# Conversion, sums and split of the second MLP's weights as one operation in seven pieces; block weights of one part per unit

## The chip, the cores and the metric

One core of one Trainium2 chip runs the whole program. The metric is device time in microseconds (us) of one execution, median of the runs; lower is better.

## What is computed

```python
x = attention(q, k, v, g_norm)            # 4608 tokens x 512
h = np.maximum(x @ w_in, 0)               # 512 x 2048
x = (s * (h * h) + b) @ w_out             # 2048 x 512
h = max(x @ w1, x @ w2, x @ w3)           # each 512 x 768
out = h @ w_out2                          # 768 x 512
```

All weights are given in 64-bit floats, everything else in 32 bits. Tokens are worked in tiles of 512 (DM and TW in the code).

## The kernel before

**Arithmetic.** A product of 32-bit numbers is made of three TensorE products of parts: each factor is split into `hi` (ACT, a copy that rounds, L179) and `lo` (DVE, factor minus hi, L180), and hi*hi, hi*lo, lo*hi are summed in PSUM. Most of the large products use Strassen's seven products in place of eight. For these the weights are combined beforehand: of four blocks `raw` come four sums `com`, and the seven blocks are split and kept as one tile of 1792 KB (`wc`).

**Weights.** A weight arrives as `raw`, 512 KB of 64-bit words for 128x512 numbers. `w_float` (L183) makes a 32-bit number of it in six instructions: ACT L187 (absolute value of the high word), DVE L188 (clamp), L189 (shift), L190 (sign), L194 (low word), L196 (sum). `plain_op` (L569) is load, these six, and a store of 256 KB to the array `wf_dr` in DRAM. `combine` (L597) with `maker` (L610) loads two such arrays back into `F`, makes the sums into `G` (L616, four instructions of 128x256), splits the seven blocks, and stores them to `wc_dr`, or keeps them. So a combined weight of the second MLP (MLP2) goes through DRAM twice. There are 24 conversions, nine combined weights `com` 0 to 8 of w1, w2, w3 and three `out` 0 to 2 of w_out2.

**Stages**, in us of the profiled execution. The opening, to about 275: attention and the first MLP (MLP1) of the first tiles by plain products, while MLP1's weights come in. To 331: a rim tile. Then three pairs of tiles (`PAIRS`): each has eight units of an H phase (`h_steps`, which makes h and squares it) and then the second product: pair 0 331 to 471 and 471 to 515 (`Second.run`), pair 1 515 to 671 and to 707, pair 2 707 to 826 and to 889. In pair 2 the second product is Strassen's as well (`Blocks.run`), with weights that `block_op` (L1528 on) makes beforehand in the H phase: F is hi plus lo of two stored chunks `wo` (L1534), G four sums (L1537), four splits, and stores to `ws_dr`; five blocks of 256 KB for each of eight q. From 889: MLP2 in units `v1` (nine for each of the token groups SUPERS) and `Output`.

**Order.** The program is written out as a sequence; a counter `clock` is moved on by `tick` as TensorE work is emitted, and `beside_of(fns, a, b)` spreads the functions fns evenly over ticks a to b from now. A store goes out a number of ticks after its data (`store(dst, src, n)`). Within `in_order` instructions keep the written order on each engine; otherwise a scheduler sets it. `U` is the length of a second product, `V` of an H phase in ticks, `ONE` that of one chunk. Loads and stores are all issued by SP, in order, and SP stands at a load whose buffer is not free.

**Preparation** is one list, `prep.todo`, worked off by `prep.step`, each step one whole operation, the load of the next one ahead of it: four steps in the rim tile, six in pair 0's H phase (MLP1's own combined weights, `pair_op`), five in pair 0's Second, 17 over pair 1, and the last four (com 0 to 2, out 2) in pair 2. `inside.step` makes com 3 to 8, out 0 and out 1, one in each unit of MLP2's first group. `block_op` runs as a whole at ticks 37 to 47 of a unit, twice in unit 0. All of these take their buffers F, G, raw and tab from one pool of three (`w2p["p"]`); `w2p["f"]`, with eleven, holds smaller tiles.

**Engines in a unit.** PE's banks are copied by ACT (`a`, `p`, `u`, `b`, all L714), which also squares in part (L460, L463) and makes gh (L483); DVE makes r (L468), the operands ops of Blocks (L1615) and gl (L484). The loads `gb` (squares from `g_dr`) feed gh in `Second.run`.

Of the kernel before, what the change touches and what calls it, by code (L numbers as in the profile page):

```python
# [22 lines left out]
P = 128  # L23
# [48 lines left out]
def fused_kernel(ctx, tc, qt, kv, kvr, g_norm, w_in, w_out, s, b, w1, w2, w3, w_out2, out):  # L72
# [110 lines left out]
    def w_float(raw, ta, tb, by_act=False, to=None):  # L183
# [3 lines left out]
        nc.scalar.activation(out=af, in_=high.bitcast(F32), func=ACTF.Abs)  # L187
# [3 lines left out]
        if by_act:  # L191
            nc.scalar.activation(out=ta, in_=low, func=ACTF.Copy, scale=2.0 ** -29)
        else:
            nc.vector.tensor_scalar(out=ta, in0=low, scalar1=2.0 ** -29, scalar2=None, op0=ALU.mult)  # L194
        to = tb if to is None else to
        nc.vector.tensor_tensor(out=to, in0=tb, in1=ta, op=ALU.add)  # L196
# [372 lines left out]
    def plain_op(src, dst, turned=False):  # L569
        got = {}  # L570

        def load():
            got["raw"] = four("raw")
            if turned:
                n = DM // Q // (P // Q)
                cut = "p (g i a) -> p g i a", "p (i g a) -> p g i a"
                to, come = (x.rearrange(c, g=n, i=P // Q) for x, c in zip((got["raw"], src), cut))
                for g in range(n):
                    dma(out=to[:, g], in_=come[:, g])
            else:  # L580
                dma(out=got["raw"], in_=src)

        def make():
            t = work("tab")
            store(dst, w_float(got["raw"], t[:, :DM], t[:, DM:], to=got["raw"][:, :DM]), 18)

        return load, make
# [22 lines left out]
    def maker(got, tile_of, dst):  # L610

        def make():
            raw, com, (tgt, whole) = got["raw"], blocks(work("G")), tile_of()

            def tt(o, x, y, op):
                nc.vector.tensor_tensor(out=com[:, o], in0=x, in1=y, op=op)  # L616

            tt(0, raw[:, 0], raw[:, 1], ALU.add)
            tt(1, com[:, 0], raw[:, 2], ALU.subtract)
            tt(2, raw[:, 3], com[:, 1], ALU.subtract)  # L620
            tt(3, raw[:, 2], raw[:, 0], ALU.subtract)
            cut = ((0, 3, raw[:, 1:4]), (3, 6, com[:, 0:3]), (6, 7, com[:, 3:4])) if whole is None else ((0, 3, raw[:, 1:4]), (3, 7, com))
            for i, (t, (a, e, src)) in enumerate(zip(tgt, cut)):
                t = t()
                hilo(t[:, 0], t[:, 1], src)
                if whole is None:
                    store(dst[:, :, a:e], t.bitcast(F32), 12 + 3 * i)
            if dst is not None and whole is not None:
                store(dst, whole.bitcast(F32), 18)

        return make
# [129 lines left out]
    big = {}  # L761
    wq = {}

    def v1(si, q, w):
# [42 lines left out]

        x = bank("x")
# [4 lines left out]
        p7 = copy(fpool("p7")[:, :n], d)  # L813
        prod(w, T, x, S2, "t2", False, False, end)
        u2 = copy(fpool("u2")[:, :n], x)
        prod(w, T, d, A22, "t4", False, False, end)
        c21 = sum_of(d, u2, "c21")
        prod(w, T, x, S1, "t1", False, False, end)
        b = copy(bank("b"), x)
        c22 = sum_of(x, p7, "c22")  # L820
        prod(w, T, a, A12, "b21", False, False, end)
        pair(keys[0], a, keys[2], c21)
        some()

# [674 lines left out]
    def com_op(i):  # L1499
        def tile_of():  # L1500
            if i < 3:
                return com_tile()
            wm[i] = t = wc_tile("wb" if i % 3 == 2 else "wa")
            return (lambda: t[:, :, 0:3], lambda: t[:, :, 3:7]), t

        (ja, ma), (jb, mb) = sides_of(i)
        return combine([wf_dr[jb][mb], wf_dr[ja][ma]], tile_of, wc_dr[i])

    def com_tile():
        return [com_part, com_part, lambda: w2p["f"].tile([P, 2, 1, HW], F32R, tag="f", name="hl")], None  # L1510

    def com_part():
        return w2p["cp"].tile([P, 2, 3, HW], F32R, tag="hl", name="hl")

    def out_op(c):
        srcs = [wf_dr[3][2 * c + k][:, o:o + HW] for o in (HW, 0) for k in range(2)]
        def tile_of():
            if c == KC - 1:
                return com_tile()
            wq[c] = t = wqp.tile([P, 2, 7, HW], F32R, tag="wq", name="wq")  # L1520
            return (lambda: t[:, :, 0:3], lambda: t[:, :, 3:7]), t

        return combine(srcs, tile_of, wo_dr.get(c))

    def block_op(q):
        with in_order():
            block_make(q)

    def block_make(q):
        raw, com = blocks(four("F")), blocks(work("G"))  # L1530
        fa, fb = wo[2 * q], wo[2 * q + 1]
        for i, w in enumerate((fa, fb)):
            hi, lo = (w[:, z].bitcast(F32).rearrange("p (n c) -> p n c", c=HW) for z in range(2))
            nc.vector.tensor_tensor(out=raw[:, 2 * i:2 * i + 2], in0=hi, in1=lo, op=ALU.add)  # L1534

        def tt(o, x, y, op):
            nc.vector.tensor_tensor(out=com[:, o], in0=x, in1=y, op=op)  # L1537

        tt(0, raw[:, 1], raw[:, 3], ALU.add)
        tt(1, com[:, 0], raw[:, 0], ALU.subtract)  # L1540
        tt(2, raw[:, 2], com[:, 1], ALU.subtract)
        tt(3, raw[:, 0], raw[:, 1], ALU.subtract)
        own = raw.bitcast(F32R)
        for k, to in enumerate((2, 0, 4, 1)):
            t = w2p["f"].tile([P, 2, HW], F32R, tag="f", name="ws") if k < 2 else own[:, 2 * k - 4:2 * k - 2]
            hilo(t[:, 0], t[:, 1], com[:, k])
# [4 lines left out]
    def wq_ops(ms):  # L1551
        return [plain_op(chunk((w1, w2, w3, w_out2)[j], m), wf_dr[j][m], j == 3) for m in ms for j in range(4)]

    conv = wq_ops(range(KM))
    prep.todo += [pair_op(0), conv[0], pair_op(1), conv[1]]
    prep.todo += [pair_op(i) for i in range(2, QF)] + conv[2:]
    com, outs = [com_op(i) for i in range(NQ)], [out_op(c) for c in range(KM // 2)]
    prep.todo += [*com[:3], outs[2]]
    inside = Ahead()
# [342 lines left out]
```

## Time and profile before

| | us |
|---|---|
| median of 3 runs | 1416.7 (1412.68 to 1416.85) |
| the profiled execution | 1415.81, span 1414.0 |
| PE, PEld busy | 1371.1, 1125.0 |
| DVE, ACT, POOL busy | 1000.4, 775.1, 10.7 |
| DMA | 310.63 MB, 63.5% of 16 engines |
| mean granted clock of PE | 0.992 |

PE is TensorE's matmuls, PEld its weight loads, which lie beside them. DVE, ACT, POOL are VectorE, ScalarE and GpSimd. The span goes from the first to the last instruction. Counts (x38) are of instructions that start in a stretch.

### The profile page before, as it was taken

To read this page: it belongs to the slowest core of one execution; us is meant where nothing else is said; L and a number is where in the kernel's file an instruction comes from. 1 tells how busy PE (TensorE), PEld (TensorE's weight loads), DVE (VectorE), ACT (ScalarE), POOL (GpSimd) and SP (SyncE) were. 2 spreads that over 40 slices of the span, in tenths; PEclk is the share of its full clock that TensorE was granted. 3 is DMA by queue.
4 is the path that set the end of the run, shared out by engine and by line. 5 is a ranking of instruction groups with operands and counts; after the bars stand their busy time and mean duration, and the time that the engine had idled before them with its cause. 6 is when DMAs were issued, how large, how long until landed. Compare 5 with 4: busy or idle time off the path is not lost.

```text
span 1414.0 us, 19588 instructions
## 1 busy us (share of the span) xinstructions
PE 1371.1 (97%) x6822; PEld 1125.0 (80%) x6822; DVE 1000.4 (71%) x1863; ACT 775.1 (55%) x1503; POOL 10.7 (1%) x40
## 2 busy tenths in 40 slices
PE   8999999999999999998988989999999999999998
PEld 6878788877888888776866767888998888888886
DVE  7998866679675776666767779598674575567555
ACT  7975554667776556664456666455453443334332
POOL 1000000000000000000000000000000000000000
PEclk9999999999999999999999999999999999999999
DMA  8486544486767857778458888558684563563542
GB/s 299 149 256 202 192 125 159 159 296 238 254 242 258 280 164 258 254 239 305 156 201 321 285 294 304 225 212 301 235 302 133 202 228 113 195 245 110 184 154 60
DMA packets 153241, 310.63 MB, mean 220 GB/s; under 512 B 62646, under 2 KB 85686, under 8 KB 144182
## 3 DMA queue, kind: packets, MB, share of 16 engines
q1 hardware_dynamic: 153136, 309.38, 63.5%
q8 instruction: 54, 0.88, 0.3%
q14 instruction: 45, 0.37, 0.1%
q10 hardware_dynamic: 6, 0.00, 0.0%
HBM read 213.91 MB, written 95.42 MB: 219 GB/s over the span
## 4 chain that ended last, share of the span: by engine, by line
PE 71%; DVE 11%; DMA 10%; ACT 4%; issue 3%; SPq 1%; DVEq 0%; POOL 0%; ACTq 0%; POOLq 0%
PE x L498 17%; PE d L498 12%; PE y L498 11%; PE o L498 9%; PE b L498 6%; PE a L498 5%; PE h L427 5%; DMA wf_dr<-raw 2%; DMA gb<-g_dr 2%; PE h L155 2%; DVE tb L155 2%; PE y L155 1%; DMA raw<-in_w_out 1%; DMA ws_dr<-F 1%; PE ops L347 1%
## 5 line engine op out<-in xcount | busy, mean ns | idle before, releaser
L498 PE MATMUL y<-gh,w 128*128 128x512 f32 x720 | 238.5, 394 | 5.6 <-ACT gh L483 4.0
L498 PE MATMUL x<-t,wc 128*128 128x512 f32 (+1 forms) x828 | 202.4, 379 | 6.6 <-ACT u L714 5.5
L498 PE MATMUL d<-t,wc 128*128 128x512 f32 (+1 forms) x828 | 201.7, 379 | 7.0 <-ACT p L714 6.3
L498 PEld LDWEIGHTS d<-t,wc 128*128 128x128 f32 x828 | 148.9, 189 | 37.8 <-ACT p L714 8.0
L498 PEld LDWEIGHTS x<-t,wc 128*128 128x128 f32 x828 | 148.6, 189 | 37.2 <-ACT u L714 6.3
L498 PEld LDWEIGHTS y<-gh,w 128*128 128x128 f32 x720 | 136.0, 190 | 35.0 <-ACT gh L483 5.5
L498 PE MATMUL y<-gl,w 128*128 128x512 f32 x360 | 142.0, 394 | 0.7 <-DVE gl L484 0.7
L498 PE MATMUL b<-b,wc 128*128 128x512 f32 (+1 forms) x414 | 101.8, 381 | 3.5 <-ACT b L714 3.3
L779 DVE TENSOR_TENSOR c<-d,u 128x512 f32<-128x512 f32 (+1 forms) x45 | 28.7, 637 | 106.2 <-PE d L498 106.2
L498 PE MATMUL a<-b,wc 128*128 128x512 f32 (+1 forms) x414 | 101.0, 376 | 0.0
L498 PE MATMUL x<-b,wc 128*128 128x512 f32 (+1 forms) x414 | 100.1, 376 | 0.0
L498 PEld LDWEIGHTS b<-b,wc 128*128 128x128 f32 x414 | 74.7, 190 | 20.4 <-ACT b L714 6.5
L498 PEld LDWEIGHTS x<-b,wc 128*128 128x128 f32 x414 | 74.3, 189 | 14.0 <-DVE r L468 0.3
L498 PEld LDWEIGHTS a<-b,wc 128*128 128x128 f32 x414 | 74.2, 188 | 13.8
L498 PEld LDWEIGHTS y<-gl,w 128*128 128x128 f32 x360 | 68.2, 190 | 14.3 <-DVE gl L484 1.6
L498 PE MATMUL o<-t,wq 128*128 128x512 f32 (+1 forms) x354 | 75.5, 369 | 0.0
L155 PE MATMUL h<-xh,w 128*128 128x512 f32 (+1 forms) x216 | 71.9, 377 | 0.6 <-ACT r L155 0.5
L498 PEld LDWEIGHTS o<-t,wq 128*128 128x128 f32 x354 | 62.4, 188 | 11.2
L774 ACT ACTIVATE a<-x 128x512 f32<-128x512 f32 (+1 forms) x45 | 24.3, 539 | 82.2 <-PE x L498 78.0
L155 PE MATMUL y<-gh,w 128*128 128x512 f32 (+1 forms) x200 | 65.2, 371 | 0.9 <-ACT st L155 0.9
L774 ACT ACTIVATE b<-x 128x512 f32<-128x512 f32 (+1 forms) x45 | 24.3, 539 | 75.9 <-PE x L498 75.9
L427 PE MATMUL h<-xh,w 128*128 128x512 f32 x192 | 64.2, 392 | 0.0
(231 smaller groups left out, 2653.6 us busy)
## 6 DMA issues: line engine op xcount, KB each, us to landing
wc<-wc_dr SPq DMA_DIRECT2D x39, 1792.0 KB, 7.5
wc<-wp_dr SPq DMA_DIRECT2D x16, 1792.0 KB, 8.8
kv<-in_kv SPq DMA_DIRECT2D x32, 512.0 KB, 5.3
wp_dr<-wc SPq DMA_DIRECT2D x8, 1792.0 KB, 7.3
gb<-g_dr SPq DMA_DIRECT2D x46, 256.0 KB, 4.9
y_dr<-st SPq DMA_DIRECT2D x42, 256.0 KB, 3.9
wc_dr<-wc SPq DMA_DIRECT2D x6, 1792.0 KB, 6.6
raw<-in_w SPq DMA_DIRECT2D x18, 512.0 KB, 5.6
```

The lines of the kernel that those rows point to most:

```text
L155: tail[eng] = call(*args, **kw).ins
L347: nc.tensor.matmul(pb, lhsT=l, rhs=r, start=(i == 0), stop=(i == 2))
L427: nc.tensor.matmul(h[:, :n], lhsT=w[:, z, kk, :], rhs=x[:, kk, o:o + n], start=(i == 0), stop=(i == 3 * KD - 1))
L498: ins = nc.tensor.matmul(*args, **kw)
L774: main["act"] = nc.scalar.activation(out=out, in_=pb, func=ACTF.Copy).ins
L779: main["dve"] = nc.vector.tensor_tensor(out=o, in0=pb, in1=t, op=ALU.add).ins
```

## The change

- `fused` takes the place of plain_op and combine for MLP2's weights: it loads two raw chunks, and has seven pieces: high and rest of the first chunk (the six instructions of w_float), the same of the second, `sums`, `his` (ACT) and `los` (DVE). Nothing goes to DRAM between. Where the result is not kept in a tile, hi and lo are written over raw and tab, with one more tile of the pool "f", and go out in five stores of 128 to 512 KB, 12 ticks on, in place of two of 768 KB and one of 256 KB.
- `phased` puts empty steps ahead of and behind the seven pieces, and `beside_of` spreads them: com 0 and 1 over pair 0's Second, com 2 to 6 over pair 1, out 2 over Blocks.run (ticks 20 to U - 24). Out 0, out 1, com 7 and 8 are spread over the units of MLP2's first group, one piece at each of six calls of `go` in a unit.
- The rim tile keeps two of the four steps, pair 0's H phase its six.
- `block_op(q)` runs in unit q, in three pieces (`sums`, `his`, `los`) at ticks 13, 23 and 33. The store of the fifth block, `ws_dr<-w`, is no longer tied behind another store.
- In Blocks: one tile of five blocks instead of two of three, fewer buffers for ops, b22's sum over t1, gates made one step earlier (`ready(k + 4)`, and one already in unit 7).

```diff
+    def fused(srcs, turned, target, dst):
+        def load():
+            for k, src in enumerate(srcs):
+                got[k] = t = four("raw")
...
+        def sums():
+            combos(blocks(got[0]), blocks(got["tab"]))
...
+        def his():
+            for hi, _, src in pieces():
+                nc.scalar.activation(out=hi, in_=src, func=ACTF.Copy)
+        def los():
+            for hi, lo, src in pieces():
+                nc.vector.tensor_tensor(out=lo, in0=src, in1=hi.bitcast(F32), op=ALU.subtract)
...
+            for z, a, e, t in ((0, 0, 2, got["to"].bitcast(F32)), (0, 2, 3, raw[:, 0:1]), (1, 0, 3, raw[:, 1:4]), (0, 3, 7, blocks(got[1])), (1, 3, 7, com)):
+                store(dst[:, z, a:e], t, 12)
+        return load, [partial(high, 0), partial(rest, 0), partial(high, 1), partial(rest, 1), sums, his, los]
...
+    def phased(op, before, behind):
+        load, fns = op
+        return [load] + [none] * before + [partial(tied_in, fn) for fn in fns] + [none] * behind
...
     def block_op(q):
...
-            store(ws_dr[to * QF + q], t.bitcast(F32), 15)
-        with tc.issue_after(stored[0]):
-            dma(out=ws_dr[3 * QF + q], in_=fb[:, :, HW:].bitcast(F32))
+                store(ws_dr[to * QF + q], t.bitcast(F32), 12)
+            store(ws_dr[3 * QF + q], wo[2 * q + 1][:, :, HW:].bitcast(F32), 12)
+        return [partial(tied_in, fn) for fn in (sums, his, los)]
...
-    beside_of([prep.step] * 4, 6, 13 * ONE)
+    beside_of([prep.step] * 2, 6, 10 * ONE)
...
-            beside_of([prep.step] * 17, 0, V + U)
+            beside_of([fn for i in range(2, NQ - 2) for fn in phased(com_op(i), 3, 4)], 0, V + U - 12)
...
-            beside_of([prep.step] * (len(prep.todo) - prep.made), 60, V + U // 4)
...
-            if blk and not end:
-                beside_of([partial(block_op, f) for f in range(q and q + 1, q + 2)], 37, 47)
+            if blk:
+                beside_of(block_op(q), 3, 33)
...
         if s == 0:
-            beside_of([prep.step] * 5, 0, U)
+            beside_of([fn for i in range(2) for fn in phased(com_op(i), 3, 4)], 0, U - 12)
+        elif blk:
+            beside_of(phased(out_op(KC - 1), 3, 0), 20, U - 24)
...
+    ops = [out_op(0, True), out_op(1, True), com_op(NQ - 2, True), com_op(NQ - 1, True)]
+    inside += [fn for op in ops for fn in phased(op, 3, 1)]
```

How the order of the instructions changes is shown at three places. First DVE in the last pair's H phase, about unit 3. Before, a com operation (L616 and the splits hl) stands ahead of the block operation:

```order
1044 L616 TENSOR_TENSOR G<-G,F 128x256
1045 L616 TENSOR_TENSOR G<-F,G 128x256
1046 L180 TENSOR_TENSOR hl<-F,hl 128x768
1047 L180 TENSOR_TENSOR hl<-G,hl 128x256
1048 L180 TENSOR_TENSOR hl<-G,hl 128x768
1049 L1534 TENSOR_TENSOR F<-w_1277 128x512
1050 L1534 TENSOR_TENSOR F<-w_1381 128x512
1051 L1537 TENSOR_TENSOR G<-F 128x256 x2
1052 L1537 TENSOR_TENSOR G<-G,F 128x256
1053 L180 TENSOR_TENSOR ws<-G,ws 128x256
```

After (L1593 is the old L1534, L1596 the old L1537, L1613 the splits, L1674 the old L1615, L477 and L493 the old L468 and L484):

```order
1035 L493 SCALAR_TENSOR_TENSOR gl<-r,cst,gh 128x512
1036 L477 ISA r<-d,u_7850 128x512
1037 L477 ISA r<-x,p_7831 128x512
1038 L493 SCALAR_TENSOR_TENSOR gl<-r,cst,gh 128x512
1039 L1593 TENSOR_TENSOR F<-w_1277 128x512
1040 L1593 TENSOR_TENSOR F<-w_1381 128x512
1041 L1596 TENSOR_TENSOR G<-F 128x256 x2
1042 L1674 TENSOR_TENSOR ops<-r 128x512 x2
1043 L1674 TENSOR_TENSOR ops<-r,ops 128x512
1044 L1596 TENSOR_TENSOR G<-G,F 128x256
1045 L1674 TENSOR_TENSOR ops<-r,ops 128x512
1046 L1596 TENSOR_TENSOR G<-F,G 128x256
```

The com operation is gone from here, the unit's own r and gl stand directly ahead of the block's first sum, and the unit's ops stand between the block's sums.

Second, SP in pair 1. Before, two conversions' stores with loads of raw and gb between:

```order
404 L176 DMA wf_dr_4_230<-raw 128x512
405 L161 DMA raw<-in_w_out 128x4x64 x4
406 L176 DMA g_dr_13_177<-r 128x512
407 L161 DMA gb<-g_dr_0_164 128x512
408 L176 DMA x_dr_131<-og 128x320
409 L161 DMA gb<-g_dr_1_165 128x512
410 L176 DMA wf_dr_4_236<-raw 128x512
411 L161 DMA raw<-in_w 128x1024
```

After, one com operation's five stores and the loads of the next:

```order
373 L176 DMA wc_dr_247<-hi 128x512
374 L176 DMA wc_dr_247<-raw 128x256
375 L176 DMA wc_dr_247<-raw 128x768
376 L176 DMA wc_dr_247<-raw 128x1024
377 L176 DMA wc_dr_247<-tab 128x1024
378 L161 DMA raw<-in_w 128x1024 x2
379 L161 DMA qt<-in_qt 128x256
380 L176 DMA x_dr_130<-og 128x64
381 L176 DMA x_dr_131<-og 128x192
382 L176 DMA g_dr_7_171<-r 128x512
383 L161 DMA wc<-wp_dr_217 128x3584
```

The single stores and loads came one by one between others; now five stores and two loads come together, and a load of a pair's weights stands behind.

Third, SP in the opening, after the change:

```order
48 L155 DMA raw<-in_w_in 128x1024
49 L155 DMA y_dr_117<-st 128x256 x2
50 L155 DMA wi_dr_201<-tb 128x512
51 L176 DMA ws_dr<-w_1077 256x1x256
52 L155 DMA raw<-in_w_out 128x1024 x2
53 L155 DMA y_dr_117<-st 128x256
54 L155 DMA wi_dr_202<-tb 128x512
55 L155 DMA raw<-in_w_in 128x1024
56 L155 DMA y_dr_118<-st 128x512 x2
57 L176 DMA ws_dr<-w_1231 256x1x256
58 L155 DMA raw<-in_w_out 128x1024
```

The stores `ws_dr<-w` (eight in all, from row 35 to 114) stood in the last pair's H phase before, from row 455 on.

## Rows read from the trace of the kernel before

**Rows 1.** The page, part 1: busy us, share, instructions.

```profile
PE 1371.1 (97%) x6822; PEld 1125.0 (80%) x6822; DVE 1000.4 (71%) x1863; ACT 775.1 (55%) x1503; POOL 10.7 (1%) x40
```

**Rows 2.** Stretches: length; PE, PEld, DVE, ACT, POOL busy (count); clock; DMA share, GB/s.

```profile
330.00:470.00 140.00, 140.00 (x775) 114.84 (x774) 100.24 (x190) 100.95 (x206) 2.40 (x8) 1.00 0.68 237
470.00:515.00 45.00, 44.85 (x197) 36.44 (x196) 34.32 (x61) 21.73 (x35) 0.00 (x0) 1.00 0.73 251
...
600.00:650.00 50.00, 45.82 (x204) 36.34 (x203) 31.99 (x63) 29.47 (x60) 0.00 (x0) 1.00 0.77 265
650.00:700.00 50.00, 44.98 (x186) 36.10 (x185) 37.51 (x64) 23.90 (x39) 0.00 (x0) 0.93 0.71 236
700.00:750.00 50.00, 45.05 (x185) 35.77 (x185) 27.98 (x53) 26.99 (x50) 0.00 (x0) 0.93 0.52 189
750.00:800.00 50.00, 43.01 (x171) 32.67 (x170) 38.07 (x74) 31.41 (x57) 0.00 (x0) 0.93 0.82 289
800.00:830.00 30.00, 27.18 (x115) 20.77 (x114) 25.82 (x50) 22.77 (x43) 0.00 (x0) 1.00 0.97 332
830.00:890.00 60.00, 57.17 (x241) 45.71 (x240) 49.31 (x78) 35.19 (x59) 0.00 (x0) 0.97 0.83 292
890.00:1000.00 110.00, 110.00 (x487) 91.12 (x486) 86.76 (x148) 54.58 (x90) 0.00 (x0) 1.00 0.62 228
```

**Rows 3.** The same view in stretches of 10 us.

```profile
670.00:680.00 10.00, 8.54 (x27) 6.88 (x28) 7.69 (x13) 5.47 (x9) 0.00 (x0) 0.67 0.95 305
...
720.00:730.00 10.00, 5.10 (x23) 3.94 (x22) 6.90 (x17) 2.80 (x8) 0.00 (x0) 0.89 0.63 256
730.00:740.00 10.00, 10.00 (x35) 7.91 (x36) 6.37 (x13) 6.44 (x12) 0.00 (x0) 0.77 0.51 169
...
830.00:840.00 10.00, 7.63 (x27) 5.78 (x26) 6.44 (x10) 3.17 (x6) 0.00 (x0) 0.83 1.00 372
...
850.00:860.00 10.00, 10.00 (x45) 8.10 (x44) 9.60 (x16) 7.29 (x13) 0.00 (x0) 1.00 0.96 319
```

**Rows 4.** Timeline of PE: start, us, line, op [idle before, releaser].

```profile
671.46 2.08 PE L498 MATMUL y<-gh,w 128*128 128x512 f32 x4 [3.63 <-ACT gh L483]
...
777.87 2.00 PE L498 MATMUL x<-t,wc 128*128 128x512 f32 x6 [3.69 <-ACT u L714]
...
833.02 0.50 PE L498 MATMUL x<-gl,wc 128*128 128x512 f32 x1 [2.37 <-DVE gl L484]
```

**Rows 5.** Waits, 700 to 830: who for whom, us in total, times, longest.

```profile
ACT ws L179 <- DVE G L1537: 13.2, 6, 5.2
...
ACT hl L179 <- DVE G L616: 7.6, 4, 5.2
```

**Rows 6.** Timeline of DVE.

```profile
727.63 0.76 DVE L1537 TENSOR_TENSOR G<-F 128x256 f32<-128x256 f32 x2 [2.80 <-DMA ws_dr<-F]
```

**Rows 7.** Waits, 590 to 690: SP's queue, then all engines.

```profile
SPq L176 <- DVE raw L196: 39.3, 9, 9.7
...
ACT gh L483 <- DMA gb<-g_dr: 10.6, 6, 4.2
```

**Rows 8.** The chain that ended last, in order of time: start, us, what.

```profile
25.39 5.68 DMA raw<-in_w_out
...
723.90 3.61 DMA ws_dr<-F
```

**Rows 9.** DVE by line and shape: busy us, mean ns, idle before.

```profile
L180 DVE TENSOR_TENSOR wc<-G,wc 128x1024 fp32r<-128x1024 f32 x14 | 17.1, 1223 | 8.9 <-ACT wc L179 8.9
...
L190 DVE SCALAR_TENSOR_TENSOR tab<-raw,tab 128x512 uint32<-128x512 uint32 x24 | 16.5, 686 | 0.3
...
L616 DVE TENSOR_TENSOR G<-F 128x256 f32<-128x256 f32 x40 | 15.3, 418 | 4.2 <-DMA ws_dr<-F 4.1
...
L188 DVE TENSOR_SCALAR tab<-tab 128x512 f32<-128x512 f32 x24 | 10.2, 424 | 26.2 <-ACT tab L187 26.1
```

**Rows 10.** The page, part 6: issues, KB each, us to landing.

```profile
wc_dr<-wc SPq DMA_DIRECT2D x6, 1792.0 KB, 6.6
```

More of the change, by code (lines that the diff above doesn't have):

```diff
@@ L194, in w_float @@
             nc.vector.tensor_scalar(out=ta, in0=low, scalar1=2.0 ** -29, scalar2=None, op0=ALU.mult)
+        for to, o in outs:
+            n = o + to.shape[-1]
+            nc.vector.tensor_tensor(out=to, in0=tb[:, o:n], in1=ta[:, o:n], op=ALU.add)
+    def w_float(raw, ta, tb, by_act=False, to=None):
         to = tb if to is None else to
[L196 removed]
+        w_abs(raw, ta)
+        w_rest(raw, ta, tb, by_act, [(to, 0)])
         return to.bitcast(F32)
@@ L595, in blocks, with combos, tt @@
         return t.bitcast(F32).rearrange("p (n c) -> p n c", c=HW)
+    def combos(raw, com):
+        def tt(o, x, y, op):
+            nc.vector.tensor_tensor(out=com[:, o], in0=x, in1=y, op=op)
+        tt(0, raw[:, 0], raw[:, 1], ALU.add)
+        tt(1, com[:, 0], raw[:, 2], ALU.subtract)
+        tt(2, raw[:, 3], com[:, 1], ALU.subtract)
+        tt(3, raw[:, 2], raw[:, 0], ALU.subtract)
     def combine(srcs, tile_of, dst):
@@ L612, in make @@
         def make():
[L613 to L629, printed above, removed]
+            raw, com, tgt = got["raw"], blocks(work("G")), tile_of()
+            combos(raw, com)
+            hilo(tgt[:, 0, 0:3], tgt[:, 1, 0:3], raw[:, 1:4])
+            hilo(tgt[:, 0, 3:7], tgt[:, 1, 3:7], com)
+            store(dst, tgt.bitcast(F32), 18)
         return make
@@ L1515, in out_op @@
[L1515 to L1523, printed above, removed]
-    def block_op(q):
[L1526 to L1546, printed above, removed]
-            store(ws_dr[to * QF + q], t.bitcast(F32), 15)
-        with tc.issue_after(stored[0]):
-            dma(out=ws_dr[3 * QF + q], in_=fb[:, :, HW:].bitcast(F32))
@@ L1551, in wq_ops, with com_op, target @@
[L1551 to L1559, printed above, removed]
-    inside.todo += [*com[3:], *outs[:2]]
-    beside_of([prep.step] * 4, 6, 13 * ONE)
+    def com_op(i, here=False):
+        def target():
+            wm[i] = wc_tile("wb" if i % 3 == 2 else "wa")
+            return wm[i]
+        (ja, ma), (jb, mb) = sides_of(i)
+        ws = w1, w2, w3
+        return fused([chunk(ws[jb], mb), chunk(ws[ja], ma)], False, target if here else None, wc_dr[i])
@@ new lines, in out_op, with target, sums, tt @@
+    def out_op(c, here=False):
+        def target():
+            wq[c] = wqp.tile([P, 2, 7, HW], F32R, tag="wq", name="wq")
+            return wq[c]
+        return fused([chunk(w_out2, 2 * c + k) for k in range(2)], True, target if here else None, wo_dr.get(c))
+    def block_op(q):
+        got = {}
+        def sums():
+            got["raw"], got["com"] = raw, com = blocks(four("F")), blocks(work("G"))
+            for i in range(2):
+                hi, lo = (wo[2 * q + i][:, z].bitcast(F32).rearrange("p (n c) -> p n c", c=HW) for z in range(2))
+                nc.vector.tensor_tensor(out=raw[:, 2 * i:2 * i + 2], in0=hi, in1=lo, op=ALU.add)
+            def tt(o, x, y, op):
+                nc.vector.tensor_tensor(out=com[:, o], in0=x, in1=y, op=op)
+            tt(0, raw[:, 1], raw[:, 3], ALU.add)
+            tt(1, com[:, 0], raw[:, 0], ALU.subtract)
+            tt(2, raw[:, 2], com[:, 1], ALU.subtract)
+            tt(3, raw[:, 0], raw[:, 1], ALU.subtract)
+        def his():
+            own = got["raw"].bitcast(F32R)
+            for k in range(4):
+                t = w2p["f"].tile([P, 2, HW], F32R, tag="f", name="ws") if k < 2 else own[:, 2 * k - 4:2 * k - 2]
+                got[k] = t
+                nc.scalar.activation(out=t[:, 0], in_=got["com"][:, k], func=ACTF.Copy)
+        def los():
+            for k, to in enumerate((2, 0, 4, 1)):
+                t = got[k]
+                nc.vector.tensor_tensor(out=t[:, 1], in0=got["com"][:, k], in1=t[:, 0].bitcast(F32), op=ALU.subtract)
+                store(ws_dr[to * QF + q], t.bitcast(F32), 12)
+            store(ws_dr[3 * QF + q], wo[2 * q + 1][:, :, HW:].bitcast(F32), 12)
+        return [partial(tied_in, fn) for fn in (sums, his, los)]
@@ L1563, in fused_kernel @@
+    prep.todo += [pair_op(i) for i in range(QF)]
+    beside_of([prep.step] * 2, 6, 10 * ONE)
     beside_of(x_of(0), 8 * ONE, 15 * ONE)
@@ L1609, in sink @@
             r = self.raw
-            a, b = ((w2p["g4"] if q < 2 else wpo).tile([P, 2, DM], F32, tag="w", name="ops") for _ in range(2))
+            a, b = ((wpo if q else w2p["g4"]).tile([P, 2, DM], F32, tag="w", name="ops") for _ in range(2))
             for nm, t in (("t1", a[:, 0]), ("t2", a[:, 1]), ("t3", b[:, 0]), ("t4", b[:, 1])):
@@ L1729, in fused_kernel @@
                 fill = blk.beside(q - 1)
-                order = (0,) * 7 if end else (0, 1, 1, 0, 1, 1, 0)
+                order = (0, 1, 1, 0, 1, 1, 0)
             elif q:
@@ L1746, in fused_kernel @@
                 step()
-                if end and k == 0 and not blk:
+                if end and blk and k == 3:
+                    blk.ready(1)
+                elif end and k == 0 and not blk:
                     after.fetch(3)
@@ L1751, in fused_kernel @@
             blk.fetch(1)
-            for fn in fill + blk.beside(QF - 1)[:2]:
+            for fn in blk.beside(QF - 1)[:2]:
                 fn()
```

106 lines of the change are left out of this document (67 added, 39 removed).

## The prediction

> **What bounds the kernel now.** I read the page first, then the busy time by stretches, then TensorE's timeline where its count falls, then the waits. By the page PE is busy 1371.1 of 1414.0 us [rows 1], so no other engine bounds the whole. The busy share hides the loss, though: what counts is how many matmuls start. In a quiet stretch, 890 to 1000 us, 487 start in 110 us, one per 0.226 us [rows 2]. At that pace 700 to 830 us (the last pair's H units, where the block weights are made) should hold 575 and holds 185 + 171 + 115 = 471: 104 are missing, **23.6 us**. 600 to 700 us (the end of the pair before) should hold 443 and holds 390: 53 missing, **12.0 us**. 830 to 890 us (Blocks.run) holds 241 of 266: **5.6 us**. The pattern to compare with is the H stage of pair 0, with one weight operation per unit: PE busy 140.00 of 140.00 us.
>
> Part of the loss is clock. From 730 to 740 us PE is busy throughout, but 35 matmuls start where 44 should, at a mean granted clock of 0.77; in the ten us before, PE was idle for 4.9 us and the clock 0.89 [rows 3]. A mean below 1.00 is a piece of the stretch at the lower of the two levels, 1.2 in place of 2.4 GHz. What it costs is the stretch times what is missing to 1.00: 1.1 + 2.3 = 3.4 us there, and 3.3 us at 670 to 680 (0.67). Both follow a long stall of PE.
>
> What PE waits for is in its timeline: 3.69 us for the copy u on ACT at 777.87, 3.63 us for gh at 671.46, 2.37 us for gl at 833.02 [rows 4]. ACT is not busy then; its copies stand behind the splits of the block weights, which wait for the sums G on DVE: 13.2 us in 6 waits and 7.6 us in 4 [rows 5]. The sums themselves wait: one G stood 2.80 us before 727.63 [rows 6], because its buffer was that of an F still being stored. So the chain is store of F, G on DVE, split on ACT, copy of u or p on ACT, PE. In pair 1 the chain is another: SP waited 39.3 us in 9 waits, at most 9.7 us, for a converted weight before it could issue its store; the loads of gb queued behind, and gh on ACT waited 10.6 us for them, 4.2 us at most [rows 7].
>
> **The change, part by part.**
>
> *The last pair's H units.* Four operations that combine weights leave this stretch (com 0 to 2, out 2), and block_op becomes three pieces per unit, with one block in unit 0 in place of two. The matmuls are the same. A removed operation is four sums of 0.418 and two splits of at most 1.223 us on DVE [rows 9], some 4.1 us; four make 16 of the 91.9 us that DVE is busy in these 130 [rows 2]. With them go the buffers they took in the pool of three, so that units 3 to 7 wait for the store of the F before at their first sum (F<-w), no longer between sums and split; unit 2's G still waits as now. That wait stays possible: between a block's last split and the next block's first sum stand four DVE operations on r and gl of about 0.69 us each (the 512-wide row of rows 9 is the nearest), 2.8 us, and a store of F landed in 3.61 us in the chain [rows 8]. I take 0 to 1.5 us of DVE's wait per unit, and that about half of it reaches PE: 7 units by 0.8 us, so that 5.6 of the 23.6 stay, **18.0 gained**. Bounds: all 23.6, the pattern of pair 0; at the other end 4, if each of seven units has a wait like the 2.80 us.
>
> *Pair 1.* Seventeen conversions of 2.64 us on DVE (three operations like L188, two like L190 [rows 9]) make way for five fused operations: two conversions, four sums and two splits, 9.4 us. 44.9 us against 47: about nothing on DVE. On SP the stores to wf_dr, each of which waited for its conversion, give way to five stores at the end of each fused operation, and the next load of raw stands directly behind them and needs the buffer that they read. A store of 1792 KB landed in 6.6 us [rows 10]; the first of the five can leave a split, 1.2 us, before the last, so SP is held some 5 us, five times: 25 us against 39.3. In proportion 7.6 of the 12.0 would stay. How long can SP be held without harm? Where it was held for up to 9.7 us, gh waited at most 4.2: 5.5 us were free. Five is under that, so I take half of the loss, **6.0 gained**, between 0 and 10.
>
> The Trainium skill, "DMA: Bandwidth & Descriptors", section "Anatomy of one DMA", puts a fixed 2.0 us on every transfer beside its bytes, and the table of the same page asks for at least 1 MiB in one; that speaks against five small stores. An estimate from that page: served one after the other they would take 14.2 us, and pair 1 would gain nothing. No row here shows five such stores together.
>
> *Pair 0's Second.* Two fused operations (18.8 us of DVE) for five conversions (13.2). DVE is idle for 10.7 of the 45 us from 470 to 515 [rows 2], which covers the 5.6. **0**; with that cover gone the 5.6 us come as waits for gl.
>
> *Blocks.run, 830 to 890.* Out 2's seven pieces move here: 9.4 us on DVE beside 49.3 of 60 [rows 2], and DVE is already busy 9.60 of the 10 us from 850 [rows 3]. It would be 58.7 of 60. At the start the stall of 2.37 us [rows 4] and the low clock behind it (0.83 from 830 to 840 [rows 3], 1.7 us) should go, since the splits of block 7 come earlier: +4. In the second half gl is then made just in time, or up to 3 us late; and the second load from ws_dr stands behind two loads of raw, one of which waits for block 7's stores: 1 to 3 us. I take **0**, between +4 and -8.
>
> *Opening.* The eight stores ws_dr<-w lose their tie to the last pair and go out in the opening, some ahead of loads of raw. The chain passes such a load there, 5.68 us [rows 8]. A 256 KB store has a seventh of a 1792 KB store's bytes, so about 0.9 us of its 6.6. One or two of the eight fall ahead of a load on the chain: **1.5 lost**, between 0 and 4.
>
> *MLP2.* Four fused operations (37.6 us) for eight combinations (32.8) over eight units; DVE has 23 us idle in 890 to 1000 alone [rows 2]. **0**; should unit 8's weights, split last, come late, up to 2 us.
>
> The smaller edits (one buffer of five blocks, b22's sum in t1's buffer, gates made one step earlier) move single DVE operations under 1 us: 0, within the bounds of Blocks.run.
>
> Sum: 18.0 + 6.0 - 1.5 = 22.5 gained. The profiled execution took 1415.8 us, so 1393.3; the median of the runs shown is 0.9 higher: **1394 us**.
>
> **The rivals.** About 0.3%, 4.2 us, is what a measurement of this kernel can tell from no change.
>
> *A, the forecast:* 1385 to 1402. For it: the com sums no longer take buffers from the blocks, and pair 0's stage with one operation per unit loses nothing. Chance 0.55.
>
> *B, the wait moves:* each block waits for the store of the one before at its first sum, and the split on ACT, with the copies behind it, waits as long as now. For it: 3.61 us of store against 2.8 us of work between. Then the last pair gives 4 and pair 1 nothing to 6, less the opening's 1.5: 1408 to 1414, say 1410. Chance 0.19.
>
> *C, Blocks.run bound by DVE:* 58.7 of 60 is a mean; if gl and out 2 meet where DVE is full, PE follows, and the 9.4 us lie on the path but for the 1.3 left over: 8 us of the gain, 1402. Against it: out 2's pieces are spread over most of the stage. Chance 0.14.
>
> *D, slower: SP held by the five stores.* Place: SP's queue in pair 0's Second and pair 1, behind each of seven com operations. If it is held for longer than the 5.5 us that were free, gb and the pair's weights come late and PE stalls as at 671.46 [rows 4]: 3.63 us and 3.3 of low clock, 6.9 us, seven times, 48 us. Less the last pair's 18 and the 12 whose place it takes: 1416.7 + 48 - 30, about 1435. It decides from five such stalls of the seven on: 34.5 is over 30 by 4.5. For it: the load directly behind the stores. Against it: the 5 us. Chance 0.09.
>
> The page's 14.2 us would be past that point.
>
> *E, the pieces do nothing:* as all of a block's pieces hang on the same buffers, they run together again when the buffer comes free, and nothing moves: 1416, give or take 3. Against it: the changed order, in which r and ops stand between the pieces. Chance 0.03.
>
> **How the numbers follow.** Faster by over 0.3%, below 1412.4: A, C and half of B, 0.79. Within: the rest of B, most of E and a little of D, 0.12. Slower: 0.09. With every term at its good end the time is 1379; the range stops little above, at 1381, and goes to 1411, which takes in C and half of B. D, E and the rest of B stay out, about 0.2.
>
> **What would show it.** Right: in the last pair's H units over 210 matmuls in each 50 us, no PE stall of over 1.5 us, ACT's waits for G under 8 us in all; in pair 1, 600 to 700 us, some 415 matmuls, and waits of SP for the stores of raw of about 5 us. Wrong: ACT waits for G as long as now, with F<-w the one that waits for the store (B); DVE full from 850 to 890 and PE waiting for gl (C); gh waiting for gb after each com operation (D).

## The result, and the profile after

The changed kernel takes 1392.08 us (median of 4 runs, 1390.93 to 1393.36) against 1416.78 of the kernel before (1412.68 to 1419.12): 0.9829 of it, 95% interval 0.9805 to 0.9853. The forecast was 1394, between 1381 and 1411. The profiled execution took 1392.0 us, its span is 1390.2.

Page of the changed kernel, busy us of each engine:

```profile
PE 1362.9 (98%) x6822; PEld 1121.3 (81%) x6822; DVE 998.1 (72%) x1873; ACT 777.6 (56%) x1507; POOL 10.7 (1%) x40
```

The same 6822 matmuls, and DVE and ACT as busy as before [rows 1]. The work has not become less; PE stands less. The view of stretches shows where (columns as in [rows 2]):

```profile
600.00:650.00 50.00, 49.65 (x226) 40.88 (x225) 41.50 (x80) 37.13 (x72) 0.00 (x0) 1.00 0.78 283
650.00:700.00 50.00, 45.60 (x194) 37.03 (x193) 27.77 (x45) 18.39 (x29) 0.00 (x0) 0.97 0.54 180
700.00:750.00 50.00, 49.89 (x217) 39.96 (x216) 35.00 (x69) 36.24 (x65) 0.00 (x0) 1.00 0.61 214
750.00:800.00 50.00, 49.95 (x218) 40.22 (x217) 37.08 (x72) 38.84 (x70) 0.00 (x0) 1.00 0.68 239
800.00:830.00 30.00, 30.00 (x135) 24.82 (x134) 28.93 (x51) 22.89 (x41) 0.00 (x0) 1.00 0.98 326
830.00:890.00 60.00, 56.64 (x245) 45.29 (x244) 45.87 (x82) 27.23 (x44) 0.00 (x0) 1.00 0.85 284
```

From 700 to 830 us 570 matmuls start where 471 did [rows 2], at a clock of 1.00 throughout. But a fixed window holds other work once the program runs ahead. So I also compare the start of the same matmul, by its place among the 6822, in the two traces; what the difference gains from one row to the next belongs to that stage. (At 303 of the places, all up to the start of MLP2, the two kernels have different products, since their order has moved; there it is the same amount of work and not the same product.)

| stage ends with the matmul that stood at | now at | difference | of this stage | forecast |
|---|---|---|---|---|
| opening, 150.05 | 152.19 | +2.14 | +2.1 | +1.5 |
| to the end of the rim tile, 331.12 | 332.05 | +0.93 | -1.2 | 0 |
| pair 0, 514.57 | 515.12 | +0.55 | -0.4 | 0 |
| pair 1, 707.09 | 699.25 | -7.84 | -8.4 | -6.0 |
| last pair's H units, 828.22 | 798.29 | -29.94 | -22.1 | -18.0 |
| Blocks.run, its start, 840.21 | 806.19 | -34.01 | -4.1 | -4 |
| Blocks.run, the rest, 890.12 | 859.25 | -30.88 | +3.1 | +4 |
| MLP2, 1060.12 | 1035.80 | -24.32 | +6.6 | 0 |
| to the end | | -24.32 | 0.0 | 0 |

In this comparison kernels with the same code up to a point still differ by some 3 us at 150 us from one execution to the next (more on this below); behind it, stages that no edit touched mostly repeat within 0.6 us; the widest difference is 1.3 (MLP2 of before_gg against MLP2 of the kernel before).

In the last pair's H units the waits of ACT for the sums G [rows 5] are down to 0.3 us in the list of waits of 690 to 812. Other waits lead it now, and one wait for a store of F is left:

```profile
DVE gl L493 <- ACT gh L492: 10.5, 10, 1.9
ACT p L776 <- PE d L507: 7.8, 8, 1.0
...
ACT r L472 <- DMA ws_dr<-F: 1.4, 1, 1.4
...
ACT ws L1608 <- DVE G L1596: 0.3, 1, 0.3
```

ACT now waits for PE's d, where PE waited for ACT's copies before.

What is left of PE's waiting is in its timeline:

```profile
661.16 0.49 PE L507 MATMUL y<-gh,w 128*128 128x512 f32 x1 [4.11 <-ACT gh L492]
...
837.54 0.50 PE L507 MATMUL d<-gl,wc 128*128 128x512 f32 x1 [1.27 <-DVE gl L180]
...
845.03 0.50 PE L507 MATMUL d<-gl,wc 128*128 128x512 f32 x1 [1.31 <-DVE gl L180]
...
851.41 0.50 PE L507 MATMUL b<-gl,ws 128*128 128x512 f32 x1 [0.72 <-DVE gl L493]
...
936.12 0.73 PE L507 MATMUL x<-b,wc 128*128 128x512 f32 x2 [0.33 <-ACT wc L627]
937.71 1.17 PE L507 MATMUL x<-b,wc 128*128 128x512 f32 x4 [0.86 <-DVE wc L631]
...
994.36 0.95 PE L507 MATMUL x<-b,wc 128*128 128x256 f32 x6 [1.47 <-DVE c L944]
```

The first is the old stall of pair 1 [rows 4], 12 matmuls earlier and somewhat longer. The next three are gl in the second half of Blocks.run. DVE has no gap there from 828 to 848, in stretches of 10 us, and in its timeline pieces of out 2 (L631) stand shortly ahead of a late gl:

```profile
828.00:838.00 10.00, 8.73 (x39) 6.94 (x38) 10.00 (x21) 8.26 (x15) 0.00 (x0) 1.00 0.82 307
838.00:848.00 10.00, 8.62 (x37) 6.48 (x36) 10.00 (x17) 3.53 (x5) 0.00 (x0) 1.00 0.94 357
```

```profile
841.62 1.22 DVE L631 TENSOR_TENSOR tab<-tab,raw 128x1024 fp32r<-128x1024 f32 x1
...
844.29 0.69 DVE L180 TENSOR_TENSOR gl<-ops,gh 128x512 fp32r<-128x512 f32 x1
```

The last ones are new, in MLP2.

### The profile page after: what moved, and what is told of

Same layout as the page of the kernel before. It is cut to its first block, busy times and chain, and to the rows that moved or that the text cites. A ratio compares the mean times of both kernels' runs of the same rounds, so it can differ in the third digit from the quotient of the medians.

```text
span 1390.2 us, 19557 instructions
## 1 busy us (share of the span) xinstructions
PE 1362.9 (98%) x6822; PEld 1121.3 (81%) x6822; DVE 998.1 (72%) x1873; ACT 777.6 (56%) x1507; POOL 10.7 (1%) x40
## 4 chain that ended last, share of the span: by engine, by line
PE 77%; DVE 10%; DMA 6%; ACT 3%; issue 2%; SPq 0%; DVEq 0%; POOL 0%; ACTq 0%; POOLq 0%
PE x L507 19%; PE y L507 16%; PE d L507 12%; PE o L507 9%; PE b L507 6%; PE a L507 6%; PE h L436 5%; DMA raw<-in_w_out 2%; DVE tb L155 2%; PE ops L356 1%; DMA raw<-in_w_in 1%; PE kvps L334 1%; DMA gb<-g_dr 1%; DMA wi_dr<-tb 1%; DVE head L155 1%
## 5 line engine op out<-in xcount | busy, mean ns | idle before, releaser
L507 PEld LDWEIGHTS y<-gl,w 128*128 128x128 f32 x360 | 68.1, 189 | 14.2 <-DVE gl L493 1.7
L835 ACT ACTIVATE a<-x 128x512 f32<-128x512 f32 (+1 forms) x45 | 24.3, 539 | 84.1 <-PE x L507 84.1
L835 ACT ACTIVATE b<-x 128x512 f32<-128x512 f32 (+1 forms) x45 | 24.3, 539 | 76.9 <-PE x L507 76.8
```

The lines of the kernel that those rows point to most:

```text
L507: ins = nc.tensor.matmul(*args, **kw)
L835: main["act"] = nc.scalar.activation(out=out, in_=pb, func=ACTF.Copy).ins
```

## The experiments

**1. The last pair: buffer, cutting, or the com operations.** Three things changed there at once. The first run gives the kernel before a buffer pool of its own for G. The room comes from two of the four buffers of ops; nothing else changes.

```diff
     def work(nm):
-        return w2p["p"].tile([P, 2 * DM], U32, tag="p", name=nm)
+        return w2p.get("gg", w2p["p"]).tile([P, 2 * DM], U32, tag="p", name=nm)
...
-            w2p["g4"] = pool("g4", 4, st=mlp1)
+            w2p["g4"] = pool("g4", 2, st=mlp1)
+            w2p["gg"] = pool("gg", 2, st=mlp1)
...
-            a, b = ((w2p["g4"] if q < 2 else wpo).tile([P, 2, DM], F32, tag="w", name="ops") for _ in range(2))
+            a, b = ((wpo if q else w2p["g4"]).tile([P, 2, DM], F32, tag="w", name="ops") for _ in range(2))
```

> The kernel before, with G alone in a pool of its own of two buffers in the last pair (F and raw keep the pool of three); room for it comes from two of the four buffers of ops. All operations stay where they are and whole. Theory (the wait of G for the store of F lost the time): the last pair's H units lose under 12 us instead of 26, the kernel takes 1398 to 1406 us, and no G waits for a DMA. Rival (the four com operations' own work and the whole block operations lost it, by holding ACT and DVE): within 4 us of before, 1413 to 1419, with ACT waiting for G as long as before.

Measured: 1400.63 us (1397.39 to 1403.7), 0.9903 of before (0.9885 to 0.9922). At the same matmuls the last pair's H units take 14.2 us less than before. Waits of 700 to 830 us in the kernel before, beside those of [rows 5]:

```profile
PE d L498 <- ACT p L714: 6.3, 3, 4.9
...
DVE G L616 <- DMA ws_dr<-F: 4.1, 2, 2.6
...
DVE G L1537 <- DMA ws_dr<-F: 3.3, 2, 2.8
```

The same view of before_gg:

```profile
ACT ws L179 <- DVE G L1537: 9.2, 5, 2.5
...
PE d L498 <- ACT p L714: 3.4, 3, 2.0
...
DVE r L468 <- DMA ws_dr<-F: 0.5, 1, 0.5
```

No sum G waits for a DMA any more. ACT still waits 9.2 us for G, but at most 2.5 at a time in place of 5.2 [rows 5], and PE stands only 3.4 us for p where it stood 6.3. So the shared buffers were the largest part, 14 of 22 us, with the four com operations still in place. (F and raw also have their three buffers to themselves in this run; it does not tell that apart from the wait of G.)

The second adds to this the block operation in three pieces, one block per unit, with the changed kernel's order of the fill work in the last unit.

```diff
-            if blk and not end:
-                beside_of([partial(block_op, f) for f in range(q and q + 1, q + 2)], 37, 47)
+            if blk:
+                beside_of(block_op(q), 3, 33)
...
-                order = (0,) * 7 if end else (0, 1, 1, 0, 1, 1, 0)
+                order = (0, 1, 1, 0, 1, 1, 0)
```

> The kernel of before_gg, and the block operation in three pieces, one block per unit and none doubled in unit 0, as in the changed kernel; the four com operations stay in the last pair's H units. Theory (three causes that add up: G's buffer about 14 us, two blocks in unit 0 and whole ones about 4, the com operations themselves the rest of the 22, about 4): 3 to 5 us below before_gg, 1395 to 1398; the last pair's H units lose 5 to 9 us. Rival (the com operations' work is the rest, and the cutting helps only where they are gone): within 1.5 us of before_gg, 1399 to 1402.

Measured: 1399.05 us (1395.77 to 1400.57). The whole time is that of the rival, the stage's that of the theory: the H units take 17.9 us less than before, 3.7 less than in before_gg, and 3.1 of that lies in the first units. Then Blocks.run gives 2.2 us back, since PE has to wait for its first loads of block weights; of PE's waits from 700 to 830:

```profile
PE x L498 <- DMA wc<-ws_dr: 4.8, 2, 3.0
```

The third goes the other way: the changed kernel with whole block operations, as before.

```diff
-            if blk:
-                beside_of(block_op(q), 3, 33)
+            if blk and not end:
+                for f in range(q and q + 1, q + 2):
+                    beside_of([lambda f=f: [fn() for fn in block_op(f)]], 37, 47)
```

> The changed kernel with block_op whole again, at ticks 37 to 47 and two in unit 0, as before; the com operations stay out of the last pair. Theory (the com operations' leaving and their buffers made the gain): 1391 to 1398 us, the last pair's H units lose under 8 us. Rival (cutting the block operation in three made it): 1402 us or more, ACT waits over 10 us for G.

Measured: 1396.06 us (1395.02 to 1397.62). At the same matmuls the H units are 4.2 us longer than in the changed kernel, and 3.4 of them come in the first 26 us, where two blocks stand in unit 0. ACT's waits for G, and PE's one stall there:

```profile
ACT ws L1608 <- DVE G L1596: 10.8, 8, 2.5
```

```profile
719.01 1.90 PE L507 MATMUL d<-t,wc 128*128 128x512 f32 x6 [2.00 <-ACT p L776]
```

The rival had the wait right (over 10 us of ACT for G) and its price wrong: eight waits of a good microsecond cost PE almost nothing; only where two blocks follow each other do they cost 3.4. The three runs add up: buffer 14.2, one block per unit in pieces 3.7 to 4.2, and 4 left for the com operations' leaving. Of the second part 3.1 to 3.4 lie in the first units, where one block stands in place of two. If that is the doubling, under 1 us is left for cutting the block in pieces; no run has one whole block per unit, so the two are not shown apart.

**2. The stores that moved into the opening.**

```diff
-            store(ws_dr[3 * QF + q], wo[2 * q + 1][:, :, HW:].bitcast(F32), 12)
+            with tc.issue_after(stored[0]):
+                dma(out=ws_dr[3 * QF + q], in_=wo[2 * q + 1][:, :, HW:].bitcast(F32))
```

> The changed kernel with the eight stores ws_dr<-w tied again behind another store, so that they leave the opening. Theory (they cost the opening about 2 us): the first 150 us come back by 1.5 to 2.1 us, the kernel takes about 1390. Rival (the opening only drifted, or the stores cost as much in the last pair): 1392, within 0.7.

Measured: 1388.98 us (1388.01 to 1390.53). The first 150 us of the profiled execution were 1.9 shorter. That could be scatter, so both kernels ran again, side by side.

> The changed kernel once more, unchanged, as the measure for the three runs beside it: 1392, between 1390.5 and 1393.5. Its first 150 us show how much the opening moves from execution to execution: the kernel before and after_out2, with the same code there as this one or without the early stores, stood 1.7 to 2.9 us earlier at the same matmul.

> The kernel of after_tie once more, beside the changed kernel on one chip. Theory (the early stores cost the opening 1.5 to 3 us): 1388.5 to 1390.5, below after_again with no overlap of most runs. Rival (the 3.1 us of after_tie were the opening's own scatter): within 1 us of after_again.

Measured: after_again 1392.21 (1388.53 to 1395.19), after_tie_again 1389.21 (1388.09 to 1389.65). Twice the tied kernel is 3.0 to 3.1 us faster in the median. The traces do not show where: in after_again the matmul of 152.19 us starts at 149.68, with the very same instructions, and in after_tie_again at 149.58. A part of what set the two executions of the changed kernel apart is clock; in the first, the stretch from 10 to 20 us has

```profile
10.00:20.00 10.00, 10.00 (x85) 6.91 (x84) 8.22 (x21) 8.13 (x22) 0.00 (x0) 0.83 1.06 381
```

a granted clock of 0.83, which is 1.7 us, where after_again and the kernel before had 1.00. Taken together, the traces show no cost of the stores here: six executions with the early stores reach this matmul at 149.3 to 152.2 us, 150.3 in the mean, and five with the tie at 149.6 to 151.2, 150.4 in the mean. So the early stores cost some 3 us by the times; that they cost it in the opening is not shown, and their place stays open.

**3. Out 2 in Blocks.run.**

```diff
-            beside_of([fn for i in range(2, NQ - 2) for fn in phased(com_op(i), 3, 4)], 0, V + U - 12)
+            beside_of([fn for op in [com_op(2), com_op(3), com_op(4), com_op(5), com_op(6), out_op(KC - 1)] for fn in phased(op, 3, 2)], 0, V + U - 12)
...
-        elif blk:
-            beside_of(phased(out_op(KC - 1), 3, 0), 20, U - 24)
```

> The changed kernel with out 2 as a sixth fused operation in pair 1 and none in Blocks.run. Theory (out 2 makes DVE the bound in the second half of Blocks.run): the 3.3 us come back there, PE's waits for gl go, pair 1 takes the sixth operation for under 1.5 us: 1389 to 1391. Rival (gl is late by its own work, or pair 1 is full): Blocks.run within 1 us of the changed kernel's, or pair 1 slower by 3 us and more: 1392 to 1396.

Measured: 1391.39 us (1388.6 to 1396.61), neither's. At the same matmuls Blocks.run is 4.6 us shorter, and PE waits for no gl there; in this rival C of the prediction had the stage right, at 4.6 in place of its 8 us. A full DVE alone does not make the wait, though: in after_out2 DVE has no gap from 828 to 848 either, and PE does not wait:

```profile
828.00:838.00 10.00, 10.00 (x46) 8.29 (x45) 10.00 (x18) 7.67 (x15) 0.00 (x0) 1.00 0.59 208
838.00:848.00 10.00, 10.00 (x46) 8.29 (x45) 10.00 (x17) 5.31 (x8) 0.00 (x0) 1.00 0.63 239
```

By the timeline of the changed kernel, what out 2 did was to stand ahead of gl. Pair 1, however, is about 5 longer. PE's stalls there:

```profile
637.81 0.41 PE L393 MATMUL mps<-sh,ones 128*128 128x320 f32 x1 [1.97 <-ACT og L359]
639.98 2.93 PE L507 MATMUL d<-t,wc 128*128 128x512 f32 x6 [1.60 <-ACT p L776]
...
655.32 0.73 PE L507 MATMUL y<-gh,w 128*128 128x512 f32 x2 [2.71 <-ACT st L531]
```

Five fused operations went into pair 1 without a stall on their account; with the sixth, all six closer packed, ACT is late three times. By the matmul that stood at 655 us this has cost 10.9 us; then 6.5 come back, because the changed kernel's stall of 661.16 is not there behind them. So about 5 is a net figure; the price of the sixth operation, with the closer packing, is about 11.

**4. The stall of pair 1.** In the changed kernel ACT waited for gb, and SP had issued that load just behind the 1792 KB of the next pair's weights. Timeline of SP, then of ACT:

```profile
650.65 0.38 SPq L161 DMA_DIRECT2D wc<-wp_dr  x1
651.09 0.45 SPq L161 DMA_DIRECT2D gb<-g_dr  x1
```

```profile
660.39 0.72 ACT L492 ACTIVATE gh<-gb,cst 128x512 fp32r<-128x512 f32 x1 [10.81 <-DMA gb<-g_dr]
```

SP's waits for the stores of raw to land, which the prediction feared there, are small. SP stands for longer at the first of the five stores, until ACT has made the hi that it takes out (500 to 690 us; the longest of these waits lies ahead of pair 1):

```profile
SPq L176 <- ACT hi L627: 25.5, 4, 13.0
...
SPq L161 <- DMA wc_dr<-raw: 4.6, 5, 1.8
```

The edit issues the first six loads of gb ahead of the next pair's weights, in pairs 0 and 1:

```diff
+        if not blk:
+            after.fetch(6)
         if s + 1 < len(PAIRS):
             wcs[0], wcs[1] = pair_load("wa", wp_dr[0]), pair_load("wa", wp_dr[1])
```

> The changed kernel with the first six loads of gb of a pair's Second issued ahead of the load of the next pair's weights, in pairs 0 and 1. Theory (gb's landing of 9.2 us behind the 1792 KB load makes PE's stall of 4.3 us in pair 1 and 1.7 us of low clock): the stall falls under 1 us, 1386 to 1388. Rival (the buffers of gb come free no earlier, or gb waits for its own store): 1391 to 1393, gh still waiting over 5 us for gb.

Measured: 1386.75 us (1384.57 to 1389.44). SP now issues gb first, ACT waits 4.3 us for it, and no stall of PE over 0.5 us is left from 640 to 662:

```profile
648.59 1.39 SPq L161 DMA_DIRECT2D gb<-g_dr  x3
650.08 0.38 SPq L161 DMA_DIRECT2D wc<-wp_dr  x1
```

```profile
651.87 1.53 ACT L492 ACTIVATE gh<-gb,cst 128x512 fp32r<-128x512 f32 x2 [4.29 <-DMA gb<-g_dr]
```

At the same matmuls 6.5 us are gained at the stall and 1.1 lost behind it, most of it where PE waits shortly for gh and gl at 664 and 668.

**5. What MLP2 lost.** PE waits for the split of com 8 at 936 to 940.

```diff
-    inside += [fn for op in ops for fn in phased(op, 3, 1)]
+    inside += [fn for op, (x, y) in zip(ops, ((3, 1), (3, 1), (3, 0), (2, 0))) for fn in phased(op, x, y)]
```

> The changed kernel with com 8's split two steps earlier (no empty step behind com 7, two in place of three ahead of com 8). Theory (unit 8 waits for the last split of its weights, 3.1 us in the trace of the changed kernel from 936 to 940): these 3 us come back, 1388.5 to 1390. Rival (the split waits for its raw loads, which are no earlier): 1391.5 to 1393.

Measured: 1391.41 us (1389.83 to 1395.14), no gain that the times show. That is near the rival's time, but not for its reason: the wait for the split is gone. Timeline of PE:

```profile
934.67 1.63 PE L507 MATMUL x<-b,wc 128*128 128x512 f32 x6 [0.73 <-DVE c L840]
...
951.42 1.85 PE L507 MATMUL o<-b,wq 128*128 128x512 f32 x7 [1.51 <-DMA wq<-wo_dr]
```

PE waits next for wq, whose load stands behind com 8's store. Before the stall DVE has little room in the changed kernel:

```profile
890.00:900.00 10.00, 10.00 (x45) 7.93 (x44) 9.80 (x22) 5.02 (x10) 0.00 (x0) 1.00 0.62 246
900.00:910.00 10.00, 10.00 (x44) 7.70 (x43) 9.90 (x17) 4.78 (x9) 0.00 (x0) 1.00 0.43 172
910.00:920.00 10.00, 9.77 (x44) 7.77 (x43) 9.05 (x18) 5.77 (x10) 0.00 (x0) 1.00 0.24 64
920.00:930.00 10.00, 10.00 (x46) 8.27 (x45) 9.84 (x18) 4.20 (x7) 0.00 (x0) 1.00 0.82 310
```

The next run takes the fourth operation out of MLP2. It is made on the kernel of the first run of part 6.

```diff
-    ops = [out_op(0, True), out_op(1, True), com_op(NQ - 2, True), com_op(NQ - 1, True)]
+    ops = [out_op(0, True), out_op(1, True), com_op(NQ - 2, True)]
...
-            beside_of([fn for i in range(2, NQ - 2) for fn in phased(com_op(i), 3, 4)], 0, V + U - 12)
+            beside_of([fn for i in (*range(2, NQ - 2), NQ - 1) for fn in phased(com_op(i), 3, 3)], 0, V + U - 12)
...
-            if i + 3 < NQ - 2:
+            if i + 3 < NQ and i + 3 != NQ - 2:
```

> The kernel of best with com 8 as a sixth operation in pair 1, loaded in MLP2 like com 0 to 6, so that MLP2's first units hold three fused operations and not four. Theory (MLP2's loss of 6.6 us comes from the fourth operation's late split, and from DVE, which is over 98% busy there): 4 to 5 us come back in MLP2; pair 1 pays 4 to 6 for the sixth operation, as with out 2: 1382 to 1386. Rival (the loss is in the order of MLP2's own instructions): MLP2 the same within 1 us, and 1387 or more.

Measured: 1394.13 us (1392.41 to 1395.85). MLP2 is 5.6 us shorter at the same matmuls, of the 6.6 lost, the wait on L944 among them; PE's waits from 890 to 1010 are now only

```profile
PE d L507 <- ACT p L835: 0.3, 1, 0.3
PE x L507 <- ACT a L835: 0.2, 1, 0.2
```

So the loss is the fourth operation's. That DVE's lack of room alone makes it is not shown. Best6 stands 6.4 us later at the start of MLP2; at that shift DVE is as busy for three of these four stretches (9.80, 9.85 and 9.10 us) and freer only in the last ten us, and PE waits for nothing over 0.3 us:

```profile
906.00:916.00 10.00, 10.00 (x45) 7.83 (x44) 9.85 (x17) 4.85 (x10) 0.00 (x0) 1.00 0.48 187
...
926.00:936.00 10.00, 10.00 (x45) 8.25 (x45) 7.93 (x13) 3.62 (x6) 0.00 (x0) 1.00 0.98 366
```

Pair 1, though, is some 8 us longer than in the changed kernel, about 14 longer than in the kernel that this one is made from, where the sixth operation was expected to cost 4 to 6. PE's waits there, 590 to 690:

```profile
PE mps L393 <- ACT og L359: 2.6, 1, 2.6
PE y L507 <- DVE st L533: 2.3, 1, 2.3
PE d L507 <- ACT p L776: 2.2, 1, 2.2
...
PE y L507 <- ACT gh L492: 1.1, 1, 1.1
```

The low clock beside these waits costs another 5.1 us: from 640 to 670 the granted clock is 0.66, 0.93 and 0.90 in stretches of 10 us, where it is 1.00 in best. This kernel no longer has the stall for gb that after_out2 got back, so here the sixth operation's price shows whole.

**6. Together.** The edits of parts 2 and 4 in one kernel:

> The changed kernel with the edits of after_tie and after_gb together. If both hold and are independent: 3.0 and 5.5 us under the changed kernel's 1392.1, 1383 to 1384.5. If one of them was scatter: 1386 or more.

Measured: 1385.21 us (six runs, 1381.98 to 1386.73), 0.9802 of before (0.9777 to 0.9828). That is 6.9 to 7.0 under the two medians of the changed kernel, and below all eight of its runs (1388.53 and more), but less than the 8.5 of both edits added; over after_gb alone the tie brings 1.5.

Then that kernel with com 8's pieces two steps earlier, as in after_com8, and its store behind the load of wq:

```diff
                 dma(out=wq[KC - 1].bitcast(F32), in_=wo_dr[KC - 1])
+                store(wc_dr[NQ - 1], wm[NQ - 1].bitcast(F32))
```

> The kernel of best with com 8's pieces two steps earlier as in after_com8, and its store behind the load of wq, on which PE stood 1.5 us there. Theory (the wait of unit 8 then does not move on to wq): 2 to 3 us under best, about 1381. Rival (wq waits for the buffers that com 8 frees, or PE waits elsewhere): within 1 us of best.

Measured: 1384.72 us (1382.34 to 1386.74). In its trace MLP2 is some 1.7 us shorter than in best's, and PE no longer waits for wq; the times overlap almost wholly, so no gain over best can be told from them.

## Why the prediction was right, and where its terms were off

The forecast of 22.5 us gained is near the 24.3 that the two traces differ by, and the mechanism is the one it named: the store of F, G, the split on ACT, the copies, PE. Its terms:

- **The last pair's H units, 18.0 gained.** They gave 22.1, near the bound of 23.6. The step "I take 0 to 1.5 us of DVE's wait per unit, and that about half of it reaches PE" was too dear: of the waits for a store of F one of 1.4 us is left. Before_gg shows the shared buffer as the main cause, by taking the sharing away alone. The prediction gave the com operations, the buffers they held and the cutting one common sum; the runs put them at about 14 for the buffer, 4 for one block per unit in pieces and 4 for the com operations. Rival B is out.
- **Pair 1, 6.0 gained.** It gave 8.4. "SP is held some 5 us, five times" is wrong: SP waits 4.6 us in all five waits, at most 1.8, for the stores of raw to land. The stores leave as their pieces come and not after the last one (in one operation hi at 642.79, tab at 645.70). Where SP does stand, the prediction did not look: at the store of hi, for ACT's split, up to 13.0 us; PE's one stall of over 0.5 us from 500 to 690 is nevertheless the one for gb. The ground of rival D, PE stalled by the five stores, did not come. The estimate that stood apart, with the stores served one after the other, does not fit the same row: SP stood 0.9 us on the mean. The Trainium skill ("DMA: Bandwidth & Descriptors", "Anatomy of one DMA") gives the fixed 2.0 us for transfers that GpSimd issues. SP issues these, and no run here has the five one after the other. No run takes the fused operations out of pair 1 alone: that they made the 8.4 is read from the traces and not tested. What was left in pair 1 was the other stall of [rows 4], for gb; after_gb shows its cause, the order of two loads on SP.
- **Blocks.run, 0, as +4 and -1 to -3 and up to -3.** It came as the parts said: 4.1 gained at the start, 3.1 lost behind it, by gl late behind out 2's pieces on DVE. The other part of the loss, the second load from ws_dr, did not come. After_out2 confirms the price of out 2 there.
- **The opening, 1.5 lost.** By the times of tied and untied kernels about 3 us, 1.5 in the combination. In the profiled execution 2.1, of which 1.7 can be a low clock that has nothing to do with the stores, and all of it lies within what the opening moves by. The sign held by the times; the place and the mechanism, a load of raw on the chain of the opening, are not shown.
- **MLP2, 0.** This is the step that failed: four fused operations at no cost, because "DVE has 23 us idle in 890 to 1000 alone", and at most 2 us if unit 8's weights come late. 6.6 came. Best6 shows whose they are: without the fourth operation 5.6 come back. By the matmuls 3.1 of the 6.6 lie around 936 to 941, where PE waits for com 8's split, 1.7 at 994, at the wait on L944, and 1.6 come little by little from 879 to 921. That the idle time was a mean is part of the answer: from 890 to 930 DVE was busy 9.1 to 9.9 of every 10 us. It is not shown to be all of it, since at the same matmuls DVE was as busy in best6 for the first 30 of these 40 us, and PE did not wait. How the wait on L944 follows, 50 us later, I cannot say.

So the closeness of the sum is luck in part: two terms were too small on the gaining side (4.1 and 2.4), and one was missing on the other (6.6). The median fell 24.7 us, of which the profiled executions show 23.8 in their spans.

## What to carry to other kernels

Look at what a late operation waits for before shortening it: 14 of the 22 us of the last pair were there for a buffer pool of its own, with the operation left whole and where it was. A queue that issues in order has its cheapest repair in the order itself: a small load that is due put ahead of a large one that is not was worth 5.5 us. And the idle time of an engine does not price an added operation: the mean over MLP2 had room and the operation cost 5.6 us, while DVE without a gap delayed nobody in after_out2. In Blocks.run it was what the added pieces stood ahead of. A run without the operation tells its price: five went into pair 1 without a stall, and the sixth cost some 11 and 14 us.

## What was not expected

The opening moves from execution to execution of the same code: the matmul that stood at 152.19 us in the profile of the changed kernel stood at 149.68 in after_again and at 149.3 to 151.7 in four other kernels with the same opening. Runs of the changed kernel spread over 6.7 us (1388.53 to 1395.19) where the tied kernel's eight spread over 2.5 (1388.01 to 1390.53); whether the early stores make the spread, or eight runs are too few, the runs do not tell.
